# Ranking the experts on the chip, and giving each rank its own product width

## The chip, the cores and the metric

One core of a Trainium2 chip runs the whole program. The metric is device microseconds (us) of one execution. The engines are TensorE (PE in the rows; PEld is its loading of weights), VectorE (DVE), ScalarE (ACT), GpSimd (POOL) and SyncE (SP), which here issues nearly all DMA transfers. One queue of instructions belongs to each engine and is worked off in order.

## The reference, cut to what matters

Three stages follow one another: masked attention (2 batches, 8 heads, 576 positions), a mixture of 8 experts with one expert per token, and a dense feed-forward layer with a rational activation.

```python
expert_idx = np.argmax(x @ w_gate, axis=1)          # 1152 tokens, 8 experts
for i in range(N):                                  # each expert keeps its first `capacity` (288) tokens
    e = expert_idx[i]
    if counts[e] < capacity: ...                    # kept, at place counts[e]
h = np.maximum(np.einsum('ecd,edf->ecf', disp, w1), 0.0)   # w1: 8 x 512 x 1024
y = np.einsum('ecf,efd->ecd', h, w2)                       # w2: 8 x 1024 x 512
out[i] = gate_w[i] * y[expert_idx[i], pos[i]]       # 0 for a token that is not kept
...
h = x @ w_in                                        # 1152 x 512 x 2048
g = (a0 + a1 h + a2 h2 + a3 h3) / (1 + |b0||h| + |b1|h2 + 1e-6)
return g @ w_out
```

How many tokens each expert keeps depends on the data. For the reference's inputs with seed 0 the counts are, in order of size, 181, 162, 158, 148, 146, 141, 111 and 105.

## The kernel before

**Attention** runs as 16 units in a software pipeline; `hooks` lists which loads are issued beside which unit. Towards its end the gate is computed (`gate_mm`, L421), each token's expert is written as a one-hot row (`oh`), and its place within its expert is counted (`rank_mm`, `rank_post`). Rows of x, already scaled by the gate, are written to a table `xd` in DRAM (`put_rows`). `index_mm` and `index` turn places into `idx`, the list of token numbers of every expert.

**Experts.** `gather(e)` fetches the rows of expert e by `idx` (two indirect DMAs on GpSimd of 96 rows each), `xpose(e)` transposes them (L669), and the loop over `e` multiplies them by 8 weight tiles of 512 KB: four of w1 (L856) and four of w2 (L871), each 8 products with a 128 x 128 block of weights and a moving operand W = 192 columns wide, whatever the count. In the trace such a float32 product leaves two records on PE, so a tile is 16 records and an expert 128. Expert e's result is copied to `yT` at the column `off[e]` where its kept tokens begin (the sum of the counts before it); what stands behind its count is overwritten by the next expert. If any count exceeds W (`flag`), a loop under `tc.If` with 64 passes computes extra windows of 128 rows; all engines read `flag` and branch.

**Weights and slots.** All weight tiles go through 35 slots of 512 KB in SBUF: 25 (`slot0`) from the start, 10 more (`slot1`) from the first expert on. `stream` is the written-out order of the loads: the 64 expert tiles in the order of the experts, and between them the 32 halves of 16 feed-forward units, which arrive as 64-bit words. `pump` issues the next loads as long as slots are free, on SP's queue; a load into a slot that was used before waits there for its last reader, and everything behind it on SP waits too. 21 loads are issued during the attention: 15 expert tiles and 6 feed-forward halves.

**Feed-forward preparation.** After each expert tile `side` runs one or two steps of `prep`. A unit takes six DVE conversions (L205, L208, L211, twice), a cast on ACT (`split_hi`) and a subtraction on DVE (`split_lo_part`, L232). Four units (`SPLIT0`) are converted in the expert stage but split inside the feed-forward stage, in four pieces of 256 columns each (`lo_piece`).

**Feed-forward.** 48 steps, each with 12 products into the hidden layer (`stage_h`), a chain of DVE and ACT operations, and 9 products into the output (`stage_o`, five steps later).

`warm` issues products of zeros that keep PE busy while it has to wait.

Of the kernel before, what the change touches and what calls it, by code (L numbers as in the profile page):

```python
# [19 lines left out]
T = B * S  # L20
# [8 lines left out]
W = 192  # L29
HW = W // 2  # L30
# [4 lines left out]
NX = -(-(T - W) // 128)  # L35
# [18 lines left out]
SPLIT0 = {1: 70, 3: 78, 5: 71, 7: 79}  # L54
# [24 lines left out]
def layout(q, k, v, moe_w_gate, moe_w1, moe_w2, moe_capacity, moe2_w_in, moe2_w_out, moe2_a, moe2_b):  # L79
# [40 lines left out]
    cf[:, F_WIN:F_WIN + NX] = W + 128 * np.arange(NX)  # L120
    cf[:, F_IOTA:F_SEL] = np.arange(16)
    cf[0:2 * E, F_SEL:F_END] = np.tile(np.eye(E), (2, 1))
# [16 lines left out]
def build(tc, qt, kt, vv, masks, cb, cf, wl, cap, wf, ab, out):  # L139
# [33 lines left out]
    stream = [(u, u) for u in range(64)] + [(4 * i + 6, (u, w)) for i, u in enumerate(ffn) for w in (0, 1)]  # L173
    stream = [k for _, k in sorted(stream, key=lambda x: x[0])]
    raw, whi, wlo = {}, {}, {}
    reserve = 0

    def pump(n=99):

        for _ in range(n):  # L180
            if not stream or len(slots.free) <= reserve:
                return
            k = stream.pop(0)
            t, _ = raw[k] = slots.take("wraw")
# [51 lines left out]
    def prepare_ops(u):  # L236
        return convert_ops(u) + ([] if u in SPLIT0.values() else [lambda: split_hi(u), lambda: split_lo_part(u, 0, 1)])

    def done(u, first=False):
        s = raw.pop(u)[1]  # L240
        slots.give(s)
        if first:

            slots.free.insert(0, slots.free.pop())
            slots.add(slot1, SLOTS[1])
# [261 lines left out]
    def index_mm(t0, t1):  # L507
        ip = late()[0][0:HW, 0:4 * E].rearrange("p (h a) -> p h a", h=2)
        for t in range(t0, t1):
            for h in range(2):  # L510
                PE.matmul(ip[:, h], lhsT=ohr[:, t, HW * h:HW * h + HW], rhs=oha[:, t].rearrange("p a e -> p (a e)"),
                          start=(t == 0 and h == 0), stop=(t == NT - 1), skip_group_check=True)

    def index():

        ip = late()[0][0:HW, 0:4 * E].rearrange("p (h a e) -> p h e a", h=2, a=2)
        ia = att.tile([HW, 2, E], F32, name="ia", bufs=1)
# [23 lines left out]
    capm = rt.tile([HW, 2], F32, name="capm")  # L541

    def capacity():

        G.tensor_copy(capf, capt.bitcast(I32)[:, 0:1])
        for h in range(2):
            G.tensor_scalar(out=capm[:, h:h + 1], in0=cft[0:HW, F_TOK:F_TOK + 1], scalar1=capf[0:HW], scalar2=-float(HW * h),
# [19 lines left out]
    for i in range(2, 17):  # L567
        hook(i, lambda i=i: pump(1 if i < 11 else 2))
# [68 lines left out]
    for f in rank_post(6, 9, rk):  # L637
        f()
# [13 lines left out]
    def gather(e):  # L652
        g = ex.tile([HW, 2, DM], F32, name="xg", bufs=1)
        for h in range(2):
            G.indirect_dma_start(out=g[:, h], out_offset=None, in_=xd[:, :],
                                 in_offset=bass.IndirectOffsetOnAxis(ap=idx[:, h, e:e + 1], axis=0))
# [4 lines left out]
    def xpose(e):  # L661
        g = xg.pop(e)
        x2 = ex.tile([128, 4, W], F32, name="x2")
        for p in range(2):
            tp = bank()[:, 0:2 * W].rearrange("p (c w) -> p c w", c=2)
            for c in range(2):
                for h in range(2):
                    d = 2 * p + c
                    PE.transpose(tp[:, c, h * HW:h * HW + HW], g[:, h, 128 * d:128 * d + 128], idf[0:HW, 0:HW])  # L669
# [8 lines left out]
    cnts = rt.tile([128, E], F32, name="cnts")  # L678

    def offsets():  # L680

        c = cnt[:, 4:]
        V.tensor_scalar(out=c, in0=rks[:, NT], scalar1=capf, scalar2=None, op0=ALU.min)
# [354 lines left out]
```

## Time and profile before

| what | value |
|---|---|
| median of 3 runs | 488.36 us (486.9 to 490.9) |
| profiled execution | 488.34 us, its span 486.6 us |
| mean granted TensorE clock | 0.964 of full |
| PE, PEld | 456.2 us (94%), 415.2 us (85%) busy |
| DVE, ACT, POOL | 324.8 (67%), 246.3 (51%), 55.2 us (11%) busy |
| DMA | 66.98 MB, mean 138 GB/s |

By the trace the attention and the routing take the first 100.2 us, the experts run from 100.2 to 272.0 us, and the feed-forward layer from there to the end. Busy shares are averages over these stages. What limits a stage is read from the chain of work that ended last and from the rates of single runs of instructions.

### The profile page before, as it was taken

The numbers are of one execution on the slowest core, as the hardware profiler recorded it, in microseconds if no ns is written. First come the engines' busy times: TensorE is split into PE (matmuls) and PEld (weight loads), VectorE is DVE, ScalarE is ACT, GpSimd is POOL, SyncE is SP. The second block draws the span as 40 slices with busy tenths as digits, with TensorE's granted clock in tenths as the row PEclk, the third lists the DMA queues.
The fourth block names the chain that finished last, engine by engine and source line by source line (L and its number), as shares of the span: only waits on it lengthen the run. The fifth ranks groups of instructions, "written<-read, shape, count | busy, mean of one in ns | idle before, by whom it ended". The sixth has DMA issues, their size and how long they took to land.

```text
span 486.6 us, 7615 instructions
## 1 busy us (share of the span) xinstructions
PE 456.2 (94%) x2781; PEld 415.2 (85%) x2782; DVE 324.8 (67%) x722; ACT 246.3 (51%) x593; POOL 55.2 (11%) x87
## 2 busy tenths in 40 slices
PE   7998777699999999999999989999989999999995
PEld 4767567589999999999999978898979999999973
DVE  2685642434475636445434699999979999959992
ACT  3785721212212121212102498778868888858881
POOL 3453420211010101101000000000020000020002
PEclk9799985699999999999999999999999999999999
DMA  8987560359985757666764000000010000010001
GB/s 287 345 315 293 186 253 22 111 200 417 387 317 182 246 206 239 206 232 203 259 223 168 2 0 2 0 1 0 2 44 23 0 0 1 1 67 0 1 0 65
DMA packets 21096, 66.98 MB, mean 138 GB/s; under 512 B 2816, under 2 KB 3200, under 8 KB 21056
## 3 DMA queue, kind: packets, MB, share of 16 engines
q1 hardware_dynamic: 19312, 60.96, 35.0%
q0 software_dynamic: 1744, 5.51, 3.8%
q8 instruction: 23, 0.38, 0.3%
q14 instruction: 17, 0.14, 0.1%
HBM read 61.73 MB, written 4.72 MB: 137 GB/s over the span
## 4 chain that ended last, share of the span: by engine, by line
PE 40%; DVE 29%; issue 5%; ACT 3%; DMA 2%; POOL 0%; POOLq 0%; another core or an unknown queue 0%; ACTq 0%
PE bank L871 17%; PE bank L856 17%; DVE p L964 5%; DVE q L963 5%; DVE glo L971 4%; DVE q L962 4%; DVE q L949 4%; DVE p L952 4%; DMA out_dram<-ob,idc 2%; PE bank L669 1%; DVE wlo L232 1%; PE bank L991 1%; DVE yl L828 1%; PE bank L989 1%; PE bank L990 1%
## 5 line engine op out<-in xcount | busy, mean ns | idle before, releaser
L871 PE MATMUL bank<-h,wraw 128*128 128x192 f32 x512 | 85.9, 327 | 0.0
L856 PE MATMUL bank<-x,wraw 128*128 128x192 f32 x512 | 84.6, 326 | 0.3 <-ACT x L670 0.3
L856 PEld LDWEIGHTS bank<-x,wraw 128*128 128x128 f32 x512 | 83.4, 190 | 0.4 <-ACT x L670 0.4
L871 PEld LDWEIGHTS bank<-h,wraw 128*128 128x128 f32 x512 | 83.3, 190 | 0.0
L919 PE MATMUL bank<-yh,whi 128*128 128x384 f32 x192 | 64.9, 338 | 1.3 <-ACT ob L995 1.3
L920 PE MATMUL bank<-yl,whi 128*128 128x384 f32 x192 | 64.7, 337 | 0.0
L921 PE MATMUL bank<-yh,wlo 128*128 128x384 f32 x192 | 64.6, 336 | 0.0
L991 PE MATMUL bank<-whi,glo 128*128 128x512 f32 x144 | 57.8, 402 | 3.1 <-DVE glo L971 3.1
L857 ACT ACTIVATE h<-bank 128x384 f32<-128x384 f32 x32 | 15.7, 491 | 84.0 <-PE bank L856 84.0
L989 PE MATMUL bank<-whi,ghi 128*128 128x512 f32 x144 | 56.9, 395 | 0.0
L990 PE MATMUL bank<-wlo,ghi 128*128 128x512 f32 x144 | 56.7, 394 | 0.0
L232 DVE TENSOR_TENSOR wlo<-wcv,whi 128x256 fp32r<-128x256 f32 (+1 forms) x28 | 21.3, 762 | 39.3 <-ACT whi L220 39.3
L960 ACT ACTIVATE r<-q,qb 128x384 f32<-128x384 f32 x48 | 29.6, 617 | 23.7 <-DVE q L949 23.7
L353 ACT ACTIVATE pt<-sc,nb 96x128 f32<-96x128 f32 (+1 forms) x88 | 30.8, 368 | 18.3 <-DVE nb L351 14.1
L919 PEld LDWEIGHTS bank<-yh,whi 128*128 128x128 f32 x192 | 36.0, 188 | 3.3 <-ACT ob L995 1.7
L991 PEld LDWEIGHTS bank<-whi,glo 128*128 128x128 f32 x144 | 27.0, 188 | 13.2 <-DVE glo L971 7.3
L920 PEld LDWEIGHTS bank<-yl,whi 128*128 128x128 f32 x192 | 36.0, 188 | 1.6
L997 POOL DMA_INDIRECT out_dram<-ob,idc x9 | 8.7, 966 | 246.0 <-ACT ob L995 243.5
L921 PEld LDWEIGHTS bank<-yh,wlo 128*128 128x128 f32 x192 | 36.0, 188 | 0.0
L948 ACT ACTIVATE q<-ah,babs 128x384 f32<-128x384 f32 x48 | 34.1, 710 | 1.6
L951 ACT ACTIVATE p<-bank,nab 128x384 f32<-128x384 f32 x48 | 31.4, 655 | 0.0
L989 PEld LDWEIGHTS bank<-whi,ghi 128*128 128x128 f32 x144 | 27.0, 188 | 4.8 <-DVE p L953 0.4
(153 smaller groups left out, 713.9 us busy)
## 6 DMA issues: line engine op xcount, KB each, us to landing
wraw<-in_wl_dram SPq DMA_DIRECT2D x64, 512.0 KB, 5.4
wraw<-in_wf_dram SPq DMA_DIRECT2D x32, 512.0 KB, 4.8
vt<-in_vv_dram SPq DMA_DIRECT2D x8, 384.0 KB, 5.4
qz<-in_qt_dram SPq DMA_DIRECT2D x8, 288.0 KB, 5.6
kz<-in_kt_dram SPq DMA_DIRECT2D x8, 288.0 KB, 5.9
xd<-xr SPq DMA_DIRECT2D x9, 256.0 KB, 2.3
xg<-xd,idx POOLq DMA_INDIRECT x16, 5.8
mkt<-in_masks_dram SPq DMA_DIRECT2D x1, 160.0 KB, 3.1
```

The lines of the kernel that those rows point to most:

```text
L353: A.activation(out=s_["pt"][:, h, i], in_=s_["sv"][h][:, i], func=AF.Exp, bias=bias[:, i:i + 1], scale=0.125, accum_out=s_["sm"][:, h, i:i ...
L856: PE.matmul(hp[:, i], lhsT=w[:, d, 128 * i:128 * i + 128], rhs=x2[:, d], start=(d == 0), stop=(d == 3), skip_group_check=True)
L871: PE.matmul(o, lhsT=w[:, f], rhs=h2[:, f], start=(f == 0), stop=(f == 7), skip_group_check=True)
L919: PE.matmul(hp, lhsT=wh, rhs=yh[:, d], start=(d == 0), stop=False)
L920: PE.matmul(hp, lhsT=wh, rhs=yl[:, d], start=False, stop=False)
L921: PE.matmul(hp, lhsT=wl, rhs=yh[:, d], start=False, stop=(d == 3))
L948: A.activation(out=q, in_=ah, func=AF.Identity, scale=babs[:, 1:2], bias=babs[:, 0:1])
L951: A.activation(out=p1, in_=hp, func=AF.Identity, scale=nab[:, 3:4], bias=nab[:, 2:3])
L960: A.activation(out=r0, in_=q, func=AF.Abs_reciprocal_sqrt, bias=qb)
L989: PE.matmul(o, lhsT=ghi[:, ts], rhs=wh, start=(f == 0), stop=False)
L990: PE.matmul(o, lhsT=ghi[:, ts], rhs=wl, start=False, stop=False)
L991: PE.matmul(o, lhsT=glo[:, ts], rhs=wh, start=False, stop=(f == NF - 1))
```

## The change

The experts are no longer worked off in the order 0 to 7 but by rank: the one that keeps most tokens first. `places` computes on DVE a place for each expert (`pos`, from pairwise comparisons of `key` = 8 x kept + priority) and a permutation matrix `pm`; `by_place` and `by_expert` carry a row of eight numbers over in either direction. Rank s has a product width of its own, `WID[s]`, from 192 down to 128. `idx` is permuted, offsets are summed in order of rank, and the flag for extra windows is set if an expert keeps more than the width of its rank.

The weights of a rank are known only once `ordi`, the list of expert numbers by rank, is known. SP reads an entry of it into a register (`values_load`) and the load takes its address from it. The stream is re-ordered: 22 halves of 11 feed-forward units come first, then the expert tiles with the halves of three more units late between them, and two units at the very end. Fourteen units are prepared in the expert stage at an even pace; what is left is done in the feed-forward stage, one step of `prep` per step, without the four pieces.

The rows of a gather are now 128 and WID - 128 instead of 96 and 96.

```diff
-W = 192
-HW = W // 2
+WID = (192, 176, 168, 160, 152, 144, 136, 128)
+W = WID[0]
...
-SPLIT0 = {1: 70, 3: 78, 5: 71, 7: 79}
+NEARLY, NPREP = 11, 14
...
-    stream = [(u, u) for u in range(64)] + [(4 * i + 6, (u, w)) for i, u in enumerate(ffn) for w in (0, 1)]
-    stream = [k for _, k in sorted(stream, key=lambda x: x[0])]
+    early = [(u, w) for u in ffn[:NEARLY] for w in (0, 1)]
+    stream = [(u, u) for u in range(64)] + [(4.4 * i + 3 if i < NPREP else 64, (u, w)) for i, u in enumerate(ffn) if i >= NEARLY for w in (0, 1)]
+    stream = early + [k for _, k in sorted(stream, key=lambda x: x[0])]
...
-                nc.sync.dma_start(out=t, in_=wl[k // 8, k % 8])
+                if k // 8 not in expert:
+                    expert[k // 8] = nc.values_load(ordi[0:1, k // 8:k // 8 + 1], engines=(ET.SP,), min_val=0, max_val=E - 1)
+                nc.sync.dma_start(out=t, in_=wl[bass.ds(expert[k // 8], 1), k % 8, :, :].rearrange("o p n -> p (o n)"))
...
+    def places():
+        return [
+            lambda: V.tensor_scalar(out=kc, in0=rks[:, NT], scalar1=capf, scalar2=None, op0=ALU.min),
+            lambda: V.scalar_tensor_tensor(out=key, in0=kc, scalar=float(E), in1=cft[:, F_PRIO:F_PRIO + E], op0=ALU.mult, op1=ALU.add),
+            lambda: V.tensor_tensor(out=gtm, in0=bc(key, 1), in1=bc(key, 2), op=ALU.is_gt),
+            lambda: V.tensor_reduce(out=pos, in_=gtm, axis=AX.X, op=ALU.add),
+            lambda: V.tensor_tensor(out=pm, in0=bc(cft[:, F_IOTA:F_IOTA + E], 2), in1=bc(pos, 1), op=ALU.is_equal),
+        ]
+    def by_place(out, x):
+        V.tensor_tensor(out=m8, in0=pm, in1=bc(x, 1), op=ALU.mult)
+        V.tensor_reduce(out=out, in_=m8, axis=AX.X, op=ALU.add)
...
         V.tensor_reduce(out=ia, in_=ip, axis=AX.X, op=ALU.add)
-        idx = rt.tile([HW, 2, E], I32, name="idx")
         for h in range(2):
-            V.tensor_scalar(out=idx[:, h], in0=ia[:, h], scalar1=capm[:, h:h + 1], scalar2=float(T), op0=ALU.mult, op1=ALU.add)
+            V.tensor_tensor(out=im[:, h], in0=pm, in1=bc(ia[:, h], 1), op=ALU.mult)
+        V.tensor_reduce(out=ib, in_=im, axis=AX.X, op=ALU.add)
+        idx = rt.tile([128, 2, E], I32, name="idx")
+        for h in range(2):
+            V.tensor_scalar(out=idx[:, h], in0=ib[:, h], scalar1=capm[:, h:h + 1], scalar2=float(T), op0=ALU.mult, op1=ALU.add)
+        iof = rt.tile([128, E], F32, name="iof")
+        by_place(iof, cft[:, F_IOTA:F_IOTA + E])
+        V.tensor_copy(ordi, iof)
...
     gather(0)
     warm(DUM2[0])
+    pump(3)
     offsets()
...
+    slots.add(slot1, SLOTS[1])
     warm(DUM2[1])
     xpose(0)
+    t, sg = slots.take("guard")
+    V.memset(t[:, 0:1], 0.0)
+    slots.free.insert(0, sg)
+    pump()
     gather(1)
...
-        if k == 0:
-            pump(1)
-        for _ in range(2 if len(prep) * 64 > nprep * (60 - k) else 1):
-            if prep and prep[0][0] in raw and slots.free:
+        n = 8 * NPREP * (k + 1) // 61
+        for _ in range(3):
+            if prep and nprep - len(prep) < n and prep[0][0] in raw and slots.free:
                 prep.pop(0)[1]()
...
-            hp = bank()[:, 0:2 * W].rearrange("p (c w) -> p c w", c=2)
+            hp = bank()[:, 0:2 * w_].rearrange("p (c w) -> p c w", c=2)
...
-    while prep:
-        prep.pop(0)[1]()
...
-        if s in SPLIT0:
-            u = SPLIT0[s]
-            split_hi(u)
-            lq.extend([lambda j=j, u=u: split_lo_part(u, j, 4) for j in range(4)])
+        if prep:
+            prep.pop(0)[1]()
+        pump()
         tick()
```

What stands on SP's queue behind the five writes to `xd` at the end of the routing is, before the change, the read of `flag` and the branch around the extra windows:

```order
L466 DMA xd<-xr 128x512 x5
L808 TENSOR_LOAD flag
L808 ISA x2
L809 COMPARE_AND_BRANCH
L810 COMPARE_AND_BRANCH
```

and after it:

```order
L468 DMA xd<-xr 128x512 x5
L191 DMA wraw<-in_wf_dram 128x1024
L194 TENSOR_LOAD ordi
L194 ISA x2
L195 ISA
L195 DMA wraw<-in_wl_dram 128x1024
L195 ISA
L195 DMA wraw<-in_wl_dram 128x1024
L855 TENSOR_LOAD flag
```

One feed-forward half and the first two expert tiles now stand ahead of the branch. The next ten expert tiles stand behind it, and the first of them waits for the memset of `guard` on DVE.

On DVE, from the last one-hot rows of the places (`ohr`) to `idx`, and on to `flag`, stands before the change:

```order
L494 TENSOR_SCALAR ohr<-cbt,r 128x192 x3
L518 TENSOR_REDUCE ia<-sc_1066 96x16
L521 TENSOR_SCALAR idx<-ia,capm 96x8 x2
L683 TENSOR_SCALAR cnt<-rks,capf 128x8
L684 TENSOR_REDUCE mxc<-cnt 128x1
L685 COPY cnts<-cnt 128x8
L686 TENSOR_SCALAR flag<-mxc 128x1
```

and after it:

```order
L529 TENSOR_SCALAR kc<-rks,capf 128x8
L530 SCALAR_TENSOR_TENSOR key<-kc,cft 128x8
L531 TENSOR_TENSOR gtm<-key 128x64
L532 TENSOR_REDUCE pos<-gtm 128x8
L533 TENSOR_TENSOR pm<-cft,pos 128x64
L552 TENSOR_REDUCE ia<-sc_1075 128x16
L554 TENSOR_TENSOR im<-pm,ia 128x64 x2
L555 TENSOR_REDUCE ib<-im 128x16
L558 TENSOR_SCALAR idx<-ib,capm 128x8 x2
L538 TENSOR_TENSOR m_128<-pm,cft 128x64
L539 TENSOR_REDUCE iof<-m_128 128x8
L561 CAST ordi<-iof 128x8
```

Eight operations now stand ahead of `idx` that did not, and three more ahead of `ordi`. Five more lead to `flag`, and behind it 16 operations follow where 11 did.

On DVE in the first steps of the feed-forward stage, from the first `yl` on, stands before the change (`wlo` in pieces of 256 columns, up to two in a step):

```order
L949 TENSOR_TENSOR q<-q,ah 128x384
L232 TENSOR_TENSOR wlo<-wcv,whi 128x256
L952 TENSOR_TENSOR p_2848<-p_2848,bank 128x384
L953 SCALAR_TENSOR_TENSOR p_2848<-p_2848,nab,bank 128x384
L971 TENSOR_TENSOR glo<-p_2784,ghi 128x384
L232 TENSOR_TENSOR wlo<-wcv,whi 128x256
```

and after it one operation of `prep` in a step:

```order
L998 SCALAR_TENSOR_TENSOR p_2926<-p_2926,nab,bank 128x384
L239 TENSOR_TENSOR wlo<-wcv,whi 128x1024
L1007 SCALAR_TENSOR_TENSOR q<-q,r_2935 128x384
L1008 SCALAR_TENSOR_TENSOR q<-q,r_2935 128x384
L1009 SCALAR_TENSOR_TENSOR p_2926<-p_2926,nab,q 128x384
L995 TENSOR_TENSOR q<-q,ah 128x384
L997 TENSOR_TENSOR p_2956<-p_2956,bank 128x384
L998 SCALAR_TENSOR_TENSOR p_2956<-p_2956,nab,bank 128x384
L1016 TENSOR_TENSOR glo<-p_2892,ghi 128x384
L212 TENSOR_SCALAR wcv<-wraw 128x512
```

Sixteen pieces are gone from these steps. In their place stand seven conversions and two subtractions of 1024 columns, and two casts on ACT where there were four: five of unit 71's six conversions are already done at the end of the expert stage.

## Rows read from the trace of the kernel before

**Rows 1.** Stretches: length, busy us of PE, PEld, DVE, ACT, POOL, clock, DMA share, GB/s.

```profile
100.20:272.00 171.80, 171.77 (x1099) 171.62 (x1099) 85.84 (x161) 33.96 (x56) 12.98 (x14) 1.00 0.70 246
```

**Rows 2.** The chain of work that ended last, 95 to 145 us: start, us, what.

```profile
95.43 3.33 DMA xg<-xd,idx
...
100.23 10.67 PE bank L856 x64
...
121.99 10.40 PE bank L856 x64
...
137.59 0.66 PE bank L669 x8
```

**Rows 3.** PE's instructions in order of time, 35 to 57 us: start, us, instruction.

```profile
35.91 2.00 PE L421 MATMUL ms<-cft,xT 128*128 128x64 f32 x16
37.75 0.67 PE L373 MATMUL tp<-cft,pt 96*128 96x96 f32 x6
...
55.09 0.66 PE L457 MATMUL ms<-cft,xT 128*128 128x128 f32 x4
55.58 0.60 PE L373 MATMUL tp<-cft,pt 126*126 126x126 f32 x4
```

**Rows 4.** All engines in order of time at the routing's end.

```profile
90.34 0.36 DVE L521 TENSOR_SCALAR idx<-ia,capm 96x8 int32<-96x8 f32 x2
...
90.36 3.60 PE L279 MATMUL bank<-wz 128*128 128x256 bf16 x16 [0.28 <-DVE ia L518]
...
91.06 0.15 DVE L686 TENSOR_SCALAR flag<-mxc 128x1 int32<-128x1 f32 x1
...
94.01 1.12 POOL L655 DMA_INDIRECT xg<-xd,idx  x1 [5.92 <-PE bank L279]
...
95.60 2.74 PE L279 MATMUL bank<-wz 128*128 128x256 bf16 x12 [1.65 <-issue]
...
100.06 0.56 DVE L670 COPY x<-bank 128x384 f32<-128x384 f32 x1 [6.86 <-PE bank L669]
```

**Rows 5.** SP's queue in order of time, and its line L188.

```profile
83.65 6.65 SPq L466 DMA_DIRECT2D xd<-xr  x5
...
L188 SPq EVENT_SEMAPHORE  x38: 17/17/28, 93.3 to 247.8; - x38
```

**Rows 6.** Issue to landing: L466 (83-92 us), L655 (93-97 us), page's issues.

```profile
DMA to landing us min/median/max: 2.0/2.3/2.8
...
DMA to landing us min/median/max: 3.3/3.3/3.3
...
wraw<-in_wl_dram SPq DMA_DIRECT2D x64, 512.0 KB, 5.4
...
xg<-xd,idx POOLq DMA_INDIRECT x16, 5.8
```

**Rows 7.** The chain in the feed-forward stage's first steps.

```profile
317.39 0.55 DVE glo L971
...
321.83 0.55 DVE glo L971
...
325.60 0.55 DVE glo L971
```

**Rows 8.** Two stretches, columns as in the first group.

```profile
99.00:100.00 1.00, 0.96 (x7) 0.78 (x6) 0.00 (x0) 0.30 (x1) 0.00 (x0) 0.70 0.00 0
120.00:130.00 10.00, 10.00 (x64) 10.00 (x63) 5.93 (x14) 2.03 (x4) 0.00 (x0) 1.00 1.03 383
```

**Rows 9.** DVE's preparation lines by form: busy us, mean ns.

```profile
L208 DVE SCALAR_TENSOR_TENSOR wcv<-wraw,wcv 128x512 int32<-128x512 int32 x32 | 22.1, 691 | 1.0
...
L232 DVE TENSOR_TENSOR wlo<-wcv,whi 128x1024 fp32r<-128x1024 f32 x12 | 14.6, 1220 | 39.3 <-ACT whi L220 39.3
L205 DVE TENSOR_SCALAR wcv<-wraw 128x512 int32<-128x512 int32 x32 | 13.5, 421 | 10.7 <-DMA wraw<-in_wf_dram 10.7
...
L232 DVE TENSOR_TENSOR wlo<-wcv,whi 128x256 fp32r<-128x256 f32 x16 | 6.7, 418 | 0.0
```

More of the change, by code (lines that the diff above doesn't have):

```diff
@@ L34 @@
 BIG = 4096.0
-NX = -(-(T - W) // 128)
+NX = -(-(T - WID[-1]) // 128)
 QB = 1.0 + 1e-6
@@ L183, in pump @@
             k = stream.pop(0)
+            loads[0] += 1
             t, _ = raw[k] = slots.take("wraw")
@@ L236, in prepare_ops, with done @@
     def prepare_ops(u):
[L237 to L245, printed above, removed]
+        return convert_ops(u) + [lambda: split_hi(u), lambda: split_lo_part(u, 0, 1)]
+    def done(u):
+        slots.give(raw.pop(u)[1])
     queue = []
@@ L507, in index_mm @@
     def index_mm(t0, t1):
-        ip = late()[0][0:HW, 0:4 * E].rearrange("p (h a) -> p h a", h=2)
+        ip = late()[0][:, 0:4 * E].rearrange("p (h a) -> p h a", h=2)
+        if t0 == 0:
+            PE.matmul(ip, lhsT=wz, rhs=wz[:, 0:4 * E].rearrange("p (h a) -> p h a", h=2), start=True, stop=False, skip_group_check=True)
         for t in range(t0, t1):
-            for h in range(2):
-                PE.matmul(ip[:, h], lhsT=ohr[:, t, HW * h:HW * h + HW], rhs=oha[:, t].rearrange("p a e -> p (a e)"),
-                          start=(t == 0 and h == 0), stop=(t == NT - 1), skip_group_check=True)
+            for h, n in enumerate((128, W - 128)):
+                PE.matmul(ip[0:n, h], lhsT=ohr[:, t, 128 * h:128 * h + n], rhs=oha[:, t].rearrange("p a e -> p (a e)"),
+                          start=False, stop=(t == NT - 1), skip_group_check=True)
@@ new lines, in build, with bc @@
+    kc, key, pos, wide, offe = (rt.tile([128, E], F32, name=x) for x in ("kc", "key", "pos", "wide", "offe"))
+    gtm, pm, m8 = (rt.tile([128, E, E], F32, name=x) for x in ("gtm", "pm", "m8"))
+    ordi = rt.tile([128, E], I32, name="ordi")
+    def bc(x, axis, n=E):
+        return x.unsqueeze(axis).to_broadcast([128, n, E] if axis == 1 else [128, E, n])
+    def places():
[6 more added lines that the diff above has]
+        ]
@@ L540, in build @@
     G.memset(off[:, 0:1], 0.0)
-    capm = rt.tile([HW, 2], F32, name="capm")
+    capm = rt.tile([128, 2], F32, name="capm")
     def capacity():
@@ L636, in build @@
         put_rows(6 + t, gps[t], (A, V, A)[t])
-    for f in rank_post(6, 9, rk):
+    post = rank_post(6, 9, rk)
+    for f in post[-1:] + post[:-1] + places():
         f()
@@ L652, in gather @@
     def gather(e):
[L653 to L656, printed above, removed]
+        g = ex.tile([128, 2, DM], F32, name="xg", bufs=1)
+        for h, n in enumerate((128, WID[e] - 128)):
+            if n:
+                G.indirect_dma_start(out=g[0:n, h], out_offset=None, in_=xd[:, :],
+                                     in_offset=bass.IndirectOffsetOnAxis(ap=idx[0:n, h, e:e + 1], axis=0))
         xg[e] = g
@@ L677, in build @@
     mxc = rt.tile([128, 1], F32, name="mxc")
-    cnts = rt.tile([128, E], F32, name="cnts")
     def offsets():
+        by_expert(wide, cft[:, F_SEL:F_END])
+        V.tensor_tensor(out=key, in0=kc, in1=wide, op=ALU.is_gt)
+        V.tensor_reduce(out=mxc, in_=key, axis=AX.X, op=ALU.max)
+        V.tensor_copy(flag, mxc)
         c = cnt[:, 4:]
-        V.tensor_scalar(out=c, in0=rks[:, NT], scalar1=capf, scalar2=None, op0=ALU.min)
-        V.tensor_reduce(out=mxc, in_=c, axis=AX.X, op=ALU.max)
-        V.tensor_copy(cnts, c)
-        V.tensor_scalar(out=flag, in0=mxc, scalar1=float(W), scalar2=None, op0=ALU.is_gt)
+        by_place(c, kc)
         V.tensor_tensor(out=cn2[:, 4:], in0=c, in1=cnt[:, 3:3 + E], op=ALU.add)
```

68 lines of the change are left out of this document (37 added, 31 removed).

## The prediction

> **What bounds the kernel now.** I read the view of stretches first. From 100.2 to 272.0 us the experts run, and PE is busy for 171.77 of 171.80 us, at the full granted clock, with DVE at half of that [rows 1]. So the product stage waits for nobody, and its length is a number of PE records times their spacing. The chain of waits confirms it: from the landing of the second gather it consists of PE alone [rows 2]. It also gives the spacing. 64 records of 192 columns take 10.40 us, which is 162.5 ns each, and 8 transposes of 96 columns take 0.66 us, 82.5 ns each [rows 2]. Both lie on one line, 2.5 ns + 0.833 ns per column. With 8 x 128 records of 162.5 ns (166.4 us) and seven times 0.66 us the stage is explained.
>
> The second question is what a record costs that is narrower than its weights. Weight loads are busy for 171.62 of the same 171.80 us [rows 1], so the busy time doesn't tell which of the two sets the pace. The gate's products do: the same kind of record, 128 x 128 float32 weights, only 64 columns. Sixteen of them go from 35.91 to 37.75 us, 115 ns each, where the line gives 56 [rows 3]. I take 115 ns as the floor that the weights set. Four transposes of 128 columns take 122 ns each (55.09 to 55.58 us) where the line gives 109 [rows 3]; they are the upper bound of the floor.
>
> At the left end of the stage `idx` was ready at 90.70 us, but the first gather started at 94.01 [rows 4]: it waited for the last write of `xd`, issued by 90.30 us and landed within 2.8 [rows 5, 6]. The second gather followed at 95.43, then its landing, the transposes and the first product at 100.23 us [rows 2].
>
> In the feed-forward stage's first steps the chain runs through DVE, and the spacing of `glo` is the length of a step: 4.43 us with two pieces of `wlo` in it, 3.77 us without [rows 7].
>
> **What the narrower products save.** By the line, with 115 ns as floor, a record costs 162.5, 149.2, 142.5, 135.8, 129.2, 122.5, 115.8 and 115 ns for the eight ranks, together 1072.5 ns against 1300. Times 128 records that is 29.1 us less. Without any floor it would be 29.9, with 122.5 ns as floor 27.3 us.
>
> The Trainium skill ("TensorE: Matmul & The Clock Gate", section on LDWEIGHTS) puts a weight load at its columns over 1.2 GHz, an estimate of 107 ns for 128 columns. The gate's 115 ns [rows 3] speaks for a little more; with 107 only the last rank would change and the sum would be 0.7 us lower.
>
> The transposes stay eight per expert, half of them 128 columns wide (109 to 122 ns), half narrower (at most 82.5): some 0.8 us for 0.66, and four fewer for the last rank. I count +0.5 us.
>
> **The start of the experts.** Eight more DVE operations stand ahead of `idx`. At the 0.18 us that the two small `idx` operations take each [rows 4] they cost 1.4 us: `idx` at 92.1 us. The gather still waits longer for the last write of `xd` (90.30 + 2.0 to 2.8 us), so this is hidden, with half a microsecond to spare; beyond that it would show one for one. `ordi` follows at 92.7 us. For `flag`, written at 91.21 us, SP was past its read and branch at 93.3 us [rows 4, 5], 2.1 us later; a register read without the branch costs at most that, so the first two expert tiles are issued between 94 and 95 us. They need 5.4 us to land [rows 6] and are there by 100.5 us.
>
> But they run beside the first gather. Alone it landed 3.3 us after its issue, beside tile loads the median was 5.8 [rows 6]. That bounds the delay of the first product at 0 and 2.5 us; two tiles and one feed-forward half are a light load, and I take 1.5. `warm` comes later too: its first batch waits for `ia`, 6 x 0.18 = 1.1 us later, `flag` is written 2.4 us later than now, and the second batch, 2.74 us long [rows 4], ends about 99.0 us in place of 98.3. Behind it PE now idles about a microsecond until the rows land. The granted clock rose only then (0.70 in the microsecond before 100 [rows 8]); if it rises later, the first tiles run at half speed. I add 0.5 us for that and 2.5 at most. Together the start costs 2.0 us, between 0.5 and 5.
>
> The third tile is issued only after `guard`, and the memset of `guard` stands on DVE behind the copy of x that ended at 100.62 us, 0.4 us after the first product [rows 4]. SP has all later loads queued behind it. At 5.4 us to landing the tile comes about 6 us after the first product, and the product wants it after two tiles, 32 x 162.5 ns = 5.2 us. With an otherwise idle queue it is faster; I take 0.3 us of waiting, between 0 and 2. After that loads gain on products: 383 GB/s at full rate [rows 8] are 1.37 us a tile, against 2.6 us for a tile of rank 0 and 1.84 of rank 7. In program order a tile is requested 11 to 13 tiles ahead at first and five ahead for the last, 9 us. The six feed-forward halves among them are the tightest place: conversions stand on DVE three or four tiles behind their request, with 5.5 to 7 us for a landing of about 5.
>
> **The feed-forward stage.** Sixteen pieces of 418 ns [rows 9] go, 6.7 us on DVE. What comes is seven conversions and two subtractions: two at 421 ns, five at 691 (the third conversion is like the second), two at 1220 [rows 9], also 6.7 us. In a saturated chain a piece lengthened a step by 0.33 us [rows 7], 0.085 less than it lasts, so sixteen cost 5.3 us, and nine longer ones cost 6.7 - 0.8 = 5.9. I count +0.5 us, between -0.5 (two casts fewer on ACT, and never two operations in one step) and +1.5. The loads during the attention are as many and as large as before, so I give that stage nothing.
>
> **The sum.** The profiled execution took 488.3 us, practically the median. 488.3 - 29.1 + 0.5 + 2.0 + 0.3 + 0.5 = 462.5 us.
>
> **Rivals.** (a) Loading weights sets the pace. PEld was busy as long as PE [rows 1]; if its floor were 162 ns, narrower products would change nothing, only the extras would be left, and the time would be 488.3 + 2.8 = 491 us. The gate's 115 ns for the same weights speak against it [rows 3]. The Trainium skill ("Perfetto Trace Analysis", section on the most contended engine) tells to judge by the busy share of weight loads rather than of products. By that rule the stage, at 99.9%, has nothing to win; that gives 491 us too. I give this 0.03.
>
> (b) The loads don't keep up. 68 tiles have to come while PE needs about 142 us less the ten that it starts ahead with, so supply limits the stage from 1.94 us a tile (270 GB/s) on. The trace shows 383 GB/s at best [rows 8], but no load whose address comes from a register. At 238 GB/s, 2.2 us a tile, the stage would be 12 us longer: 474 us. At 2.5 us a tile the whole gain would be gone. Chance 0.07.
>
> (c) Slower, because an expert outgrows its rank. The sixth rank has 144 columns for 141 kept tokens by the reference's arithmetic. Four more would set `flag`, and the loop of 64 passes would run, each with a register read and a branch on every engine. PE's one such read now shows as the gap from 93.96 to 95.60 us [rows 4], 1.64 us; 64 of them are 105 us, so at least 567 us. Before, the limit was 192 columns for 181, and the trace shows no window. Rounding on the chip can move single tokens, hardly four: 0.02.
>
> **How the numbers follow.** The forecast, with its own uncertain start, has 0.87; its low end is 488.3 - 29.9 + 0.5 + 0.5 - 0.5 = 459, its high end 488.3 - 27.3 + 0.8 + 5 + 2 + 1.5 = 470. The range goes from 458.5 to 471, which holds the forecast and the mild part of (b). Within 1% means 483.5 to 493.2 us, about what a measurement of this kernel can tell from no change. Faster by more: the forecast, most of (b) and what is left over, 0.94. Within 1%: (a), 0.03. Slower: (c) and the hard end of (b), 0.03.
>
> **What would show it.** Products of rank 0 at 162.5 ns a record and falling in equal strides of 13 or 7 ns to about 115 with the last two ranks nearly alike; an expert stage of about 143 us; PE idle in it only at the third tile, if at all. First product at 102 us. `glo` every 3.8 to 4.9 us in the first eleven feed-forward steps, 3.77 after them. The prediction is wrong if records of 128 columns stay above 125 ns, if PE shows waits for `wraw`, or if the clock is below full after 104 us.

## The result, and the profile after

The changed kernel takes 467.88 us, median of 4 runs (467.66 to 469.43), beside 489.63 us for the kernel before (4 runs, 486.9 to 493.42). The ratio is 0.956 with a 95% interval from 0.949 to 0.963: faster, and within the predicted range, but 5.4 us above the forecast of 462.5. The profiled execution took 469.43 us with a span of 467.3; the other three lie 1.5 us lower.

First the view of stretches of the changed kernel, with the columns of [rows 1], from the first to the last expert product.

```profile
105.17:252.58 147.41, 147.41 (x1095) 144.93 (x1095) 81.45 (x153) 32.81 (x58) 12.73 (x13) 0.99 0.79 272
```

The expert stage lasts 147.41 us where it lasted 171.8, and PE is still busy for all of it. So the products themselves became shorter, and PE never waited for a load of weights. Its first product starts at 105.17 us, though, and not at 100.23 as in [rows 2].

The chain of waits shows both. Here it is for the changed kernel: start, us, what.

```profile
105.24 12.73 PE bank L908 x64
117.98 5.20 PE bank L923 x32
123.18 1.09 PE bank L712 x8
124.27 5.40 PE bank L923 x32
129.67 9.55 PE bank L908 x64
...
150.03 9.12 PE bank L908 x64
...
169.98 8.69 PE bank L908 x64
...
188.61 8.27 PE bank L908 x64
...
206.38 7.84 PE bank L908 x64
...
223.27 7.41 PE bank L908 x64
...
234.39 0.44 PE bank L712 x4
...
238.54 7.14 PE bank L908 x64
```

The first 64 records of ranks 1 to 7 take 9.55, 9.12, 8.69, 8.27, 7.84, 7.41 and 7.14 us: 149.2, 142.5, 135.8, 129.2, 122.5, 115.8 and 111.6 ns a record, in strides of 13.3 and 6.7 ns. That is the line of 2.5 ns + 0.833 ns a column, down to 128 columns. Two other things stand out. Rank 0's first 64 records take 12.73 us, where the next 32 of the same width take 5.20 us, so 64 should take 10.40. And eight transposes take 1.09 us, not the 0.8 of the prediction; after them the second half of a rank's output products is 0.2 us longer than the first (5.40 beside 5.20).

Next the stretch ahead of the first product, all engines in order of time.

```profile
92.51 3.56 PE L281 MATMUL bank<-wz 128*128 128x256 bf16 x16 [0.78 <-DVE ia L552]
...
93.20 0.37 DVE L558 TENSOR_SCALAR idx<-ib,capm 128x8 int32<-128x8 f32 x2
...
94.89 1.18 POOL L697 DMA_INDIRECT xg<-xd,idx  x1 [5.98 <-DMA wraw<-in_wf_dram]
95.01 0.15 DVE L727 CAST flag<-mxc 128x1 int32<-128x1 f32 x1
95.17 11.12 SPq L195 DMA_DIRECT2D wraw<-in_wl_dram  x3
...
96.39 0.90 POOL L697 DMA_INDIRECT xg<-xd,idx  x1 [0.32 <-DVE off L732]
...
100.67 2.72 PE L281 MATMUL bank<-wz 128*128 128x256 bf16 x12 [4.60 <-PEq L856]
...
103.18 2.06 PE L712 MATMUL bank<-cft,xg 128*128 128x128 f32 x8
...
105.84 0.06 DVE L868 MEMSET guard<- 128x1 f32 x1
```

PE ends its first batch of zeros at 96.07 us and then idles for 4.60 us, where it idled for 1.65 before [rows 4], and what released it is its own queue at L856, the branch on `flag`. Here is that line's view: queue, instruction, count, ns of one, first and last start.

```profile
L856 DVEq EVENT_SEMAPHORE  x2: 21/21/21, 99.3 to 99.4; - x2
L856 PEldq EVENT_SEMAPHORE  x2: 51/51/51, 100.4 to 100.6; - x2
...
L856 PEldq COMPARE_BRANCH  x1: 4553/4553/4553, 95.8 to 95.8; - x1
```

PE's branch takes 4553 ns. In the kernel before that record was 353 ns, but it isn't the whole way. Here are PE's read of `flag` before, its events at the branch before, and its read after:

```profile
L808 PEldq TENSOR_LOAD <-flag x1: 511/511/511, 91.3 to 91.3; - x1
```

```profile
L809 PEldq EVENT_SEMAPHORE  x2: 51/51/51, 94.0 to 94.1; - x2
...
L809 PEldq COMPARE_BRANCH  x1: 353/353/353, 91.9 to 91.9; - x1
```

```profile
L855 PEldq TENSOR_LOAD <-flag x1: 489/489/489, 95.2 to 95.2; - x1
```

From the read to PE's next product it was 4.3 us before (91.3 to 95.60 [rows 4], the last 1.4 of them with no wait that the profile shows) and it is 5.5 us after (95.2 to 100.67). The larger change is how much of this way lies under the first batch of zeros: 2.7 us before (to 93.96), 0.9 us after (to 96.07).

The first gather's landing, by the view of its line in this stretch:

```profile
DMA to landing us min/median/max: 6.9/6.9/6.9
```

That one value is the first half's: it landed at 101.8 us, 6.9 us after its issue instead of 3.3 [rows 6]. The view has none for the second half, but from 102 to 104 us no DMA moves anything (second row below), so its rows were in about a microsecond before PE finished its second batch (103.39). Two delays of nearly the same length lie side by side, and PE's is the longer one. Last, the granted clock (the last column but two) in steps of 2 us:

```profile
98.00:100.00 2.00, 0.00 (x0) 0.00 (x0) 0.18 (x1) 0.00 (x0) 0.00 (x0) 0.83 1.00 387
...
102.00:104.00 2.00, 2.00 (x11) 1.36 (x9) 0.00 (x0) 0.00 (x0) 0.00 (x0) 0.50 0.00 0
...
106.00:108.00 2.00, 2.00 (x8) 2.00 (x7) 0.00 (x0) 0.00 (x0) 1.36 (x2) 0.50 0.52 139
108.00:110.00 2.00, 2.00 (x9) 2.00 (x8) 0.00 (x0) 0.00 (x0) 0.00 (x0) 0.61 1.09 356
110.00:112.00 2.00, 2.00 (x15) 2.00 (x14) 1.72 (x3) 0.49 (x1) 0.00 (x0) 1.00 0.88 256
```

From 100 to 108 us it is 0.50, the level of 1.2 GHz. It fell while PE stood idle, and the products of rank 0 began on it: 8 records in the 2 us from 106, 15 in the 2 us from 110. In the feed-forward stage the chain gives these `glo`:

```profile
289.64 0.55 DVE glo L1016
294.00 0.55 DVE glo L1016
298.37 0.55 DVE glo L1016
302.14 0.55 DVE glo L1016
```

Steps of 4.36 and 4.37 us with one step of `prep` in each, then 3.77 us; before they were 4.43 and 3.77 [rows 7]. From the last expert product to the end the stage takes 467.3 - 252.58 = 214.72 us, before 486.6 - 271.95 = 214.65.

### The profile page after: what moved, and what is told of

The parts are those of the page before. It is cut to its first block, busy times and chain, and to the rows that moved or that the text cites. A ratio compares the mean times of both kernels' runs of the same rounds, so it can differ in the third digit from the quotient of the medians.

```text
span 467.3 us, 7780 instructions
## 1 busy us (share of the span) xinstructions
PE 433.1 (93%) x2778; PEld 390.4 (84%) x2779; DVE 326.4 (70%) x728; ACT 243.7 (52%) x593; POOL 55.0 (12%) x86
## 4 chain that ended last, share of the span: by engine, by line
PE 35%; DVE 31%; issue 6%; ACT 3%; DMA 2%; POOL 0%; POOLq 0%; ACTq 0%
PE bank L908 15%; PE bank L923 14%; DVE p L1009 5%; DVE q L1008 5%; DVE glo L1016 5%; DVE q L1007 4%; DVE q L995 4%; DVE p L997 4%; PE bank L712 2%; DMA out_dram<-ob,idc 2%; DVE yl L881 1%; PE bank L1035 1%; PE bank L1034 1%; PE bank L1033 1%; DVE p L998 1%
## 5 line engine op out<-in xcount | busy, mean ns | idle before, releaser
L908 PE MATMUL bank<-x,wraw 128*128 128x192 f32 (+7 forms) x512 | 72.0, 302 | 0.0
L923 PE MATMUL bank<-h,wraw 128*128 128x192 f32 (+7 forms) x512 | 71.5, 298 | 0.0
L908 PEld LDWEIGHTS bank<-x,wraw 128*128 128x128 f32 x512 | 71.0, 194 | 0.1
L923 PEld LDWEIGHTS bank<-h,wraw 128*128 128x128 f32 x512 | 69.1, 190 | 0.2
L909 ACT ACTIVATE h<-bank 128x384 f32<-128x384 f32 (+7 forms) x32 | 13.9, 433 | 78.2 <-PE bank L908 78.2
L1005 ACT ACTIVATE r<-q,qb 128x384 f32<-128x384 f32 x48 | 29.6, 617 | 25.5 <-DVE q L995 25.5
L239 DVE TENSOR_TENSOR wlo<-wcv,whi 128x1024 fp32r<-128x1024 f32 x16 | 19.6, 1223 | 25.6 <-ACT whi L227 24.5
```

The lines of the kernel that those rows point to most:

```text
L908: PE.matmul(hp[:, i], lhsT=w[:, d, 128 * i:128 * i + 128], rhs=x2[:, d], start=(d == 0), stop=(d == 3), skip_group_check=True)
L923: PE.matmul(o, lhsT=w[:, f], rhs=h2[:, f], start=(f == 0), stop=(f == 7), skip_group_check=True)
L1005: A.activation(out=r0, in_=q, func=AF.Abs_reciprocal_sqrt, bias=qb)
```

## The experiments

The question was not why the kernel became faster; the chain shows that. It was why it stayed 5 us behind the forecast, the profiled execution 7 us: its first product came 4.9 us later than before, rank 0's records took 2.3 us more than at full clock, and the transposes 2 us more, where the forecast had 2.0 for the first two together and 0.5 for the third. The first theory was that the loads that now run beside the gather and the branch make both slow. The rival was that `flag` comes too late for the branch, which then has nothing to lie under. To compare executions whose attention ends at different times, I count from the last ACT copy of `rks`, the last step ahead of `places` (89.12 us before, 89.95 after): the first product comes 11.11 us later before the change, 15.22 after it. Four later executions with the same start gave 15.7 to 16.2 us, so differences of some tenths tell nothing here.

**The loads alone, in the kernel before.** One feed-forward half is issued after the first batch of zeros, two expert tiles behind `offsets`, through the `guard` slot.

```diff
     gather(0)
     warm(DUM2[0])
+    pump(1)
     offsets()
+    t, sg = slots.take("guard")
+    V.memset(t[:, 0:1], 0.0)
+    slots.free.insert(0, sg)
+    pump(2)
```

> The kernel before, with one feed-forward half and two expert tiles issued where the changed kernel issues them: between the first gather and the branch around the extra windows (the two tiles wait for a memset on DVE after the offsets). Nothing else is changed, and the ranking is absent. Theory A, that loads beside the branch hold up PE's branch and the gather: PE's compare-and-branch grows from 353 ns to 2 us or more, the gather lands 5 to 7 us after its issue in place of 3.3, the first product moves from 100.2 us to 102.5 to 105 us, and the kernel is 2 to 6 us slower. Rival B, that the late branch of the changed kernel comes from its later flag and longer chain on DVE: branch under 0.6 us, first product within 1 us of 100.2, time the same.

491.86 us, ratio 1.008 (1.005 to 1.012). In this execution the gather's and the branch's lines show:

```profile
DMA to landing us min/median/max: 5.8/6.3/6.8
```

```profile
L814 PEldq EVENT_SEMAPHORE  x2: 51/51/51, 92.4 to 92.6; - x2
...
L814 PEldq COMPARE_BRANCH  x1: 352/352/352, 90.3 to 90.3; - x1
```

The gather lands 2.5 to 3.5 us later beside the loads, the first product comes 13.12 us after `rks` in place of 11.11, and the first 64 records take 12.35 us in place of 10.67, on a clock that was 0.50 from 102 to 104 us. Together 3.7 us, and the medians differ by 3.9. But the record of PE's branch is as short as before (352 ns), and from the read of `flag` to PE's next product it is 5.1 us where it was 4.3. So the loads explain the slow gather; of the late second batch they explain 0.8 us at most.

**The loads behind the branch, in the changed kernel.** `pump(3)` moves behind the `If`.

```diff
     warm(DUM2[0])
-    pump(3)
     offsets()
...
                     extra_window(e, e * NX + w)
+    pump(3)
     slots.add(slot1, SLOTS[1])
```

> The changed kernel with its three early loads issued behind the branch in place of ahead of it. Theory A: PE's compare-and-branch falls from 4.55 us to under 1 us, the gather lands 3.3 to 5 us after its issue in place of 6.9, the first product comes 1.5 to 3.5 us earlier than 105.2 us although the first tile is requested 2 us later, and the time is 463 to 466 us. Rival B: the branch stays at about 4.5 us, and with the tiles later the kernel is 1 to 3 us slower than the changed one, 469 to 471 us. Rival C, that the first tile is then late: first product at 105 us or later, waiting for wraw.

467.33 us, ratio 0.955 (0.947 to 0.963), the time of the changed kernel. The two halves of the gather landed after 5.4 and 4.5 us, yet PE's branch still took 4305 ns, although the first load was issued at 99.30 us and the branch began at 97.9. PE's second batch set the start again: first product 14.94 us after `rks`. That is little to gain from the shorter of two delays that lie side by side.

**All ranks 192 columns wide.**

```diff
-WID = (192, 176, 168, 160, 152, 144, 136, 128)
+WID = (192,) * 8
```

> The changed kernel with 192 columns for every rank: ranking, loads by register and re-ordered stream stay, only the narrower products are undone. By the spacing of the records (162.5 ns against 1069 ns for the eight ranks together) the expert stage should be 29.6 us longer: about 497 us, 1 to 2 per cent slower than the kernel before. If supply of weights or another wait took part of the gain in the changed kernel, the difference is smaller, 20 to 27 us, with PE idle in the changed kernel's expert stage.

498.77 us, ratio 1.020 (1.012 to 1.028). All ranks take 10.40 us for 64 records at full clock (the first 64 of rank 0, again on a low clock, 12.30). Against the changed kernel that is 30.9 us more, by the records 29.6. Against the kernel before it is 10.8 us more: the price of everything in the change but the widths.

**A longer first batch of zeros,** 32 products instead of 16, to cover the branch.

```diff
-DUM2 = (16, 12)
+DUM2 = (32, 12)
```

> The changed kernel with 32 in place of 16 products of zeros ahead of the branch, so that PE is busy until about 99.5 us and takes its branch when the early loads have mostly landed. Theory A: the branch itself falls under 1.5 us, the first product stays within 1 us of 105 us because the gather lands at 103 us in any case, and the granted clock is full 2 to 4 us earlier, which brings 1 to 2 us: 466 us. Rival B (branch late for another reason): the branch stays 4.5 us long from 99.5 us on, first product at 108 us or later, 470 us or more.

468.65 us, ratio 0.960 (0.951 to 0.968). The batch ended at 97.68 us, but the branch became longer with it (6232 ns), and PE idled 4.95 us all the same. The first product came 16.92 us after `rks`, 0.8 to 1.7 us later than in the executions of the unaltered start, and the first 64 records took 10.67 us, 2 us less than in the changed kernel. The two cancelled, and neither theory had said so.

**The flag earlier.** `wide`, `key`, `mxc` and `flag` are computed right behind `places`, ahead of `ia`.

```diff
+    by_expert(wide, cft[:, F_SEL:F_END])
+    V.tensor_tensor(out=key, in0=kc, in1=wide, op=ALU.is_gt)
+    V.tensor_reduce(out=mxc, in_=key, axis=AX.X, op=ALU.max)
+    V.tensor_copy(flag, mxc)
...
```

> The changed kernel with flag computed right after the places, ahead of the work on idx, instead of after it. Theory (the jump behind the read of flag costs PE some 4 to 5.5 us in every kernel, in the kernel before it lies under the first batch of warm-up products, after the change flag comes too late to hide it): flag is written near 93.4 us, about 1.8 us earlier, PE's idle time between the two warm-up batches falls from 4.6 to about 2 to 3 us, the second batch starts near 98.5; but idx comes 0.9 us later and the gather, which lands 6 to 7 us after its issue beside the tile loads, now decides alone, so that the first product stays within 1 us of 105.2 and the time is 467 to 469 us. Rival (PE's long branch has another cause than the lateness of flag, for instance the queue of the loads): the gap stays 4.5 us or more wherever flag stands, and the time is 468 to 469 us.

467.28 us, ratio 0.957 (0.951 to 0.964). PE's idle time fell to 2.29 us and its second batch began at 99.39, the first as the theory had it, the second 0.9 us later. In the branch's view and the timeline of this kernel one sees what it waited for now:

```profile
L856 PEldq EVENT_SEMAPHORE  x2: 51/51/51, 97.8 to 97.9; - x2
L856 DVEq EVENT_SEMAPHORE  x2: 21/21/21, 99.3 to 99.4; - x2
...
L856 PEldq COMPARE_BRANCH  x1: 3505/3505/3505, 94.2 to 94.2; - x1
```

```profile
99.39 2.74 PE L281 MATMUL bank<-wz 128*128 128x256 bf16 x12 [2.29 <-DVEq L856]
101.92 0.63 PE L718 MATMUL bank<-cft,xg 128*128 128x128 f32 x2
103.18 0.97 PE L718 MATMUL bank<-cft,xg 64*128 64x64 f32 x6 [0.62 <-DMA xg<-xd,idx]
```

PE was through at 97.9 us, but it started only as DVE came through the same place, which had the small operations of `offsets` queued ahead of it. Then the gather's second half was last, 6.0 us after its issue. First product 14.38 us after `rks`: 0.8 to 1.8 us gained, one delay uncovered by the other. The theory's jump of 4 to 5.5 us "in every kernel" comes near when the whole way from the read of `flag` to PE's next product is counted: 4.3 us in the kernel before, 4.6 to 7.2 us in the twelve executions with the change's order.

**A quiet start:** the early flag, the loads behind the `If` (as above), and batches of 24 and 4 zeros.

> The kernel of the early flag with the first feed-forward half and expert tiles issued only behind the branch, and warm-up batches of 24 and 4 products instead of 16 and 12. Theory (loads beside gather and jump, and a jump that is not covered, make the start 3 us late; the clock falls because PE is idle meanwhile): the jump lies under the warm-up products, the gather lands in 4.5 to 5 us, the first product comes 2 to 3 us earlier than in the changed kernel counted from the last write to the table of x, the clock is full by 106 us; 463 to 465 us. Rival (what is gained at the gather is lost because the first tiles now land after the transposes): the first product waits for its weights, and the time is 467 us or more.

468.91 us, ratio 0.961 (0.954 to 0.968): the theory's 463 to 465 us was missed. The gather still took 5.7 and 5.9 us to land, probably because SP was through the branch early and issued the first of the loads at 93.41 us, before the gather (93.65). PE had nothing to do while it waited for the rows, the clock fell to 0.50 at 102 us, and rank 0's first 64 records took 13.37 us. PE was busy all through them, so the wait for weights that the rival expected isn't there either. The first product came 14.61 us after `rks`.

**The transposes in groups of one shape.** The change had put two of 128 rows and two narrower ones in turn.

```diff
-        for p in range(2):
-            tp = bank()[:, 0:2 * w].rearrange("p (c w) -> p c w", c=2)
-            for h, n in enumerate((128, w - 128)):
-                for c in range(2 if n else 0):
-                    d = 2 * p + c
-                    PE.transpose(tp[:, c, h * 128:h * 128 + n], g[0:n, h, 128 * d:128 * d + 128], idf[0:n, 0:n])
+        tps = [bank()[:, 0:2 * w].rearrange("p (c w) -> p c w", c=2) for p in range(2)]
+        for h, n in enumerate((128, w - 128)):
+            for d in range(4 if n else 0):
+                PE.transpose(tps[d // 2][:, d % 2, h * 128:h * 128 + n], g[0:n, h, 128 * d:128 * d + 128], idf[0:n, 0:n])
...
```

> The changed kernel with an expert's eight transposes in another order: the four of 128 rows first, then the four narrower ones, instead of two and two alternating. Theory (going from one shape to the other costs extra): a group of eight takes 0.8 us instead of 1.05, seven groups save 1.5 to 2 us, 466 to 466.5 us. Rival (every float32 transpose takes some 130 ns whatever its rows, because its load of 128 columns takes that): a group stays at 1.05 us and the time within 0.5 us of the changed kernel's.

467.47 us, ratio 0.959 (0.952 to 0.966), too wide an interval for so small a step. The chain shows it:

```profile
121.29 0.81 PE bank L710 x8
122.10 5.40 PE bank L922 x32
```

The seven groups take 0.81, 0.81, 0.80, 0.79, 0.78, 0.78 and 0.44 us, 5.2 together, where the changed kernel has 6.8. So it was the order of the shapes that cost, 0.25 us per expert, and not the single transpose. The 0.2 us behind them stay.

**Widths below 128.**

```diff
-WID = (192, 176, 168, 160, 152, 144, 136, 128)
+WID = (192, 176, 160, 128, 112, 96, 80, 64)
...
```

> The changed kernel with the widths 192, 176, 160, 128, 112, 96, 80 and 64; rows of an expert beyond the width of its rank are left out of the computation, and the extra windows are kept off. Theory (loading 128 x 128 float32 weights sets a floor of 111 to 115 ns a record): the records of 128 columns take 109 to 112 ns, those of 112, 96, 80 and 64 columns all 111 to 115 ns. Rival (the line of 2.5 ns plus 0.833 ns a column goes on, and the gate's 115 ns have another reason): 95.8, 82.5, 69 and 56 ns.

457.43 us in one run; it leaves rows out, so only its records are read. The chain of ranks 3 and 7 (128 and 64 columns):

```profile
169.32 7.14 PE bank L908 x64
...
228.03 7.13 PE bank L908 x64
235.17 7.15 PE bank L923 x64
```

The groups of 64 records from 128 columns down take 111.4 to 111.7 ns a record, those of 64 columns too. The floor exists and the last rank stands exactly on it; widths below 128 would save nothing at the products. The Trainium skill ("TensorE: Matmul & The Clock Gate", section on LDWEIGHTS) gives an estimate of 107 ns for loading 128 columns; the run shows 4% more. That the loading of columns sets the floor is not shown: no run varies the weights of the products, and the transposes of the kernel before load 128 columns too, over 96 rows, and take 82.5 ns a record [rows 2].

**All together:** early flag, loads behind the `If`, grouped transposes, batches of 24 and 14 zeros.

> The early flag, loads behind the branch, grouped transposes, and warm-up batches of 24 and 14 products, so that PE works until the gathered rows land. Theory (the start is late by the jump, the crowded gather and the clock that falls while PE idles, the transposes by the switching of shapes): the clock stays full over the first products, whose 64 records take 10.4 to 11 us, the first product comes 14 to 14.5 us after the last write of idx's predecessor, the places, i.e. 2 to 3 us earlier than in the changed kernel, the transposes take 0.8 us per expert; together 4 to 5 us less than the changed kernel, ratio to the kernel before 0.946 to 0.950. Rival (what these parts save is taken back by loads that come later): PE waits for weights in rank 0 and the time is within 1.5 us of the changed kernel's, 0.953 to 0.957.

465.17 us, ratio 0.952 (0.947 to 0.957), between what theory and rival had said. The transposes gained their 1.6 us. The first product came 14.96 us after `rks`, only 0.3 to 1.2 us earlier than in the executions of the unaltered start, and the clock fell again (0.50 from 106 to 108 us, 12.35 us for the first 64 records): the gather took 6.5 us, PE had nothing left to do at 101.5, and the last rows came at 104.1.

**One load fewer beside the gather.** As above, but the feed-forward half that was issued ahead of the first expert tiles comes four tiles later.

```diff
     stream = early + [k for _, k in sorted(stream, key=lambda x: x[0])]
+    stream.insert(26, stream.pop(21))
...
-    pump(3)
+    pump(2)
```

> As the kernel with all parts together, and the feed-forward half that is issued between the writes to the table of x and the expert tiles comes four expert tiles later, so that two loads and not three run beside the first gather. Theory (the gather's landing grows with the loads beside it): the first gather lands in 4 to 4.7 us in place of 5 to 5.9, and the first product comes another 0.5 to 1 us earlier. Rival (two loads are as bad as three, since the tiles alone fill the DMA engines while the gather runs): landing 5 to 6 us and no gain.

463.56 us, ratio 0.951 (0.946 to 0.956), and 461.03 in the profiled execution. Its chain, and its clock:

```profile
101.33 10.67 PE bank L908 x64
112.00 5.20 PE bank L923 x32
```

```profile
98.00:100.00 2.00, 1.26 (x12) 0.96 (x10) 0.00 (x0) 0.00 (x0) 0.00 (x0) 1.00 0.69 250
100.00:102.00 2.00, 1.13 (x8) 0.99 (x9) 0.56 (x2) 0.48 (x1) 0.96 (x1) 1.00 0.05 18
```

The gather landed after 4.6 and 5.4 us, at 98.0 and 100.3, the first half before PE's second batch ended (98.83). PE idled 1.04 us at most in this stretch, the clock stayed full, rank 0's first records took what they should, and the first product came 13.78 us after `rks`. The intervals of this kernel and of the one before it overlap, and the profiled execution is the fastest of its six: what one load fewer gains is read from one trace each, the times don't show it.

**The gather alone.** The changed kernel without `pump(3)`: all three loads wait behind `guard`, that is, until the rows are transposed.

```diff
     warm(DUM2[0])
-    pump(3)
     offsets()
```

> The changed kernel with the three loads that run beside the first gather held back until its rows are transposed: nothing else moves on the DMA queues while the gather runs. Theory (the loads beside it make the gather slow): it lands in 3.2 to 3.6 us with its 128 and 64 rows, as with 96 and 96 rows in the kernel before; tile 0 then lands only 5 to 6 us after the transposes and the first product comes later, near 107 us. Rival (the gather is slow because of its new shape, 128 rows in the first half): it lands in 5 us or more although it is alone.

473.87 us in one run; PE waited 8.28 us for the first tile, as it had to. The views of the gather and of the branch:

```profile
DMA to landing us min/median/max: 4.1/4.7/5.3
```

```profile
L855 PEldq EVENT_SEMAPHORE  x2: 51/51/51, 97.8 to 98.0; - x2
...
L855 PEldq COMPARE_BRANCH  x1: 4252/4252/4252, 93.5 to 93.5; - x1
```

Neither theory is right alone. With nothing beside it the half of 128 rows lands after 5.3 us and the half of 64 rows after 4.1, in the old shape both did after 3.3. Beside the loads the executions of the unaltered start show 4.8 to 6.9 us for the first half and 6.3 to 6.6 for the second, so the loads add up to 1.6 us to the one and about 2.3 to the other. And the branch takes 4.25 us with no load in flight, so the loads aren't what makes its record long.

**The changed kernel again,** beside the last three.

> The changed kernel as it is, beside the two kernels above on the same chip, so that differences of some 2 us can be read. All theories: ratio to the kernel before 0.954 to 0.960.

468.91 us, ratio 0.962 (0.958 to 0.967), a little above what was expected; first product 16.15 us after `rks`, branch 5482 ns, first 64 records 12.28 us. The interval of the kernel with one load fewer ends at 0.956, below where this one begins: that version beats both kernels, by 5.4 us in the medians of this comparison. Its profiled execution shows where: 2.4 us at the first product, 1.6 at rank 0's records, 1.6 at the transposes.

## Why the prediction was right in sign and 5 us too low

**Products.** Predicted -29.1 us by the line with a floor of 115 ns. The records of ranks 1 to 7 give -29.6 us (1300 - 1069 ns, times 128), and at equal widths the time came back. The reading that PE's record spacing, and not the busy weight loads, sets the pace was right. The gate's 115 ns, from which the floor was taken, was 3.5 ns too high. The rule of the Trainium skill ("Perfetto Trace Analysis", section on the most contended engine), as the prediction used it, would have given 491 us and doesn't hold here: PEld was busy for 99.9% of the stage [rows 1] and the stage still became 24 us shorter. The same section of the Trainium skill sets MFU, the share of the peak arithmetic that a kernel reaches, beside the busy share of weight loads; the prediction took the busy share alone.

**Rivals.** (a) and (b) are refuted by the stage itself: PE is busy for 147.41 of 147.41 us at 272 GB/s, so loads with an address from a register kept up. The sum of (b) had a slip: 68 tiles at 2.2 us are 149.6 us against its own 132, 17.6 us longer and not 12. No extra window ran, so (c) is out too. The third tile's 0.3 us didn't appear either; `guard` was written at 105.84 us, 0.7 us after the first product, and the tile came in time.

**Feed-forward stage.** Predicted +0.5, measured +0.07 us.

**The transposes** were mis-sized: predicted +0.5 us, 0.8 per expert. Shapes in groups would have taken just that; in turn they take 1.05, which is +2.15 us for the seven groups, and +0.8 for the products right behind them.

**The start** is the step that failed. Predicted +2.0 us, at most 5; it cost 4.1 us from `rks` to the first product and 2.1 at rank 0's records (12.73 us, before 10.67), 6.2 together. That the eight operations ahead of `idx` would be hidden was right: the gather was issued 4.89 us after `rks` before and 4.94 after. Three sentences were wrong. "Alone it landed 3.3 us after its issue" held for 96 and 96 rows; the new shape alone takes 5.3 and 4.1, and its first half beside the loads 6.9. "The second batch ends about 99.0 us" took PE's way through the branch from a row in which most of it lay under the first batch. From the read of `flag` to PE's next product it was 4.3 us before, of which 1.64 were to be seen; after the change it is 5.5 us, of which 4.60 are to be seen, and the batch ended at 103.39. And "if the clock rises later, the first tiles run at half speed" was put at 0.5 us where 2.3 came (against full clock), close to the 2.5 given as its most: PE idled for 4.60 us between the batches, not for one behind them. One of the prediction's own signs of being wrong came true with it: the clock was below full after 104 us, until about 109.5.

That the time still fell into the range is partly luck. The start alone went past its worst case; what kept the sum inside is that the products came out better than their worst case and the third tile and the feed-forward stage cost nothing.

The sum with measured terms, for the profiled execution: 488.34 + 0.83 (its attention ended later) - 29.6 + 2.15 + 0.8 + 4.1 + 2.1 + 0.07 + 0.4 (outside the span) = 469.2 us, and 469.43 was measured.

**What stays open.** Why the record of PE's branch is 3.3 to 6.2 us after the change and 0.35 before. Not the loads (4.25 us without any, 0.35 with them in the old order), and not the lateness of `flag` alone (3.5 us with `flag` early). The whole way from the read to the next product differs much less, 4.3 and 5.1 us in the two executions of the old order and 4.6 to 7.2 in the twelve of the new, so the short record is a part of a long way. What the way is made of is open. The Trainium skill ("Runtime: NRT & Kernel Launch", section on instruction fetch) says that a taken branch to a target outside the pages at hand waits for a DMA to fetch it. No run here shows whether that happens: between the read and the next product three packets of instruction queues start before the change and four after it. Why 64 rows alone land later (4.1 us) than 96 did (3.3) is open too, since a gather of 96 and 96 rows wasn't run in the changed kernel, and `offsets` behind the `If`, which would bring DVE through earlier, wasn't tried.

## What to carry to other kernels

A stage in which both products and weight loads read 100% busy can still shrink: take the ns per record at two widths from the trace, draw the line, and look for a short record of the same weights that shows the floor. When the price of a step is read from a trace, ask what covered it there: a jump of 4.3 us with 2.7 of them under a batch of products shows as 1.6, and shows as more as soon as its operand comes later. Where two delays end close together, take both away before judging either; each alone left the time where it was, both with the clock gave 4 us in one execution of each kernel.

## What the runs showed of the hardware

- Behind a flag that all engines read, PE went on when both it and DVE were through: in twelve executions with the change's order its second batch began within 0.2 us of the last event there on PE or DVE, whichever was later (99.4 and 99.39 us with the early flag, where DVE was last). It didn't wait for SP, whose last event there came at 102.5 us in the changed kernel, after PE's 100.67.
- Float32 transposes, four of 128 rows and four of 48 to 8, cost 0.10 us each in groups of one shape and 0.13 us when the two shapes take turns in twos.
- The granted clock's recovery varied: with nearly the same start (second batch of zeros at 100.67 and 100.76 us) it was full at about 109.5 us in one execution and about 105 in another (the one with grouped transposes), 2 us of difference in rank 0's first 64 records, which are the same instructions in both.
- Two indirect gathers of 0.39 MB together (96 rows each) landed after 3.3 us alone and after 6.8 and 5.8 us with three plain loads of 512 KB beside them, in one execution of each.
